# The rows of maxima turned by VectorE instead of TensorE, sent in eight transfers, with 24 tiles of exponentials and a new issue table

## The chip, the cores and the metric

One core of a Trainium2 chip runs the whole program in one launch. The metric is device time in microseconds, from the first to the last instruction with the little that lies around them. A run of this kernel repeats to within a few tenths of a microsecond; a difference of 0.2% (about 3.4 us) is the smallest that counts here.

## The reference, cut to what matters

```
xn  = layernorm(x)                                  # 2048 tokens x 512
q, k, v = split(xn @ wqkv)                          # 32 heads of 16
p   = softmax(q k^T / 4)                            # 2048 x 2048 per head, not causal
s   = (p v) @ wo
g   = silu( (silu(xn @ w1) * (xn @ w3)) @ w2 )      # 512 -> 1792 -> 512
out = x + s * g
```

All is float32. The weights are drawn large, so the scores are large, and the softmax needs each row's maximum taken off before the exponential.

## The kernel before, in words

**Shape of the work.** After a prologue (layer norm, q/k/v, some 160 us) the attention runs in 32 phases (`PHASES`): 16 pairs of heads, and for each pair two halves of 1024 queries. The gate (w1, w3, w2) is worked in between. Each operand that needs it is split in a high and a low part, and three products stand for one exact one. What a phase does:

- **maxima**, "m" (line 388): 64 products of 128 queries by 512 keys. VectorE reduces each to one maximum per query (line 390). A phase's maxima are needed one phase ahead, so they are worked out during the phase before.
- **rows**, `max_rows` (lines 393 to 414): the 16 columns of maxima of the phase (two heads by eight blocks of 128 queries, 128 partitions) have to become rows of `qs`, the tile that holds the queries: partition 62 of each half tile takes the negated maximum's high part, partition 63 its low part. The keys' tile holds ones there, so the next product takes the maximum off by itself.
- **exponentials**, "s" (line 626): 64 products of 128 keys by 512 queries, now with the rows of maxima in the contraction (64 partitions, `KR`; the maxima use 62, `KM`). ScalarE's Exp moves each to an SBUF tile `pt` (line 629), of which there are `PTS` = 23.
- **values**, "v" (line 639): four `pt` tiles times the values with a column of ones, added up in one PSUM bank `pv`. 16 of these in a phase.

**Lanes.** The products m, s and the gate's f (line 857) contract over 64 partitions. TensorE takes two at once, one on partitions 0 to 63 (lower-case letter, one head), the other on 64 to 127 (capital). Such a half product is one slot of a lane. A "v", an "o" of the end and the transpose of line 403 need the whole array, so both lanes have to end first.

**The order of the work** is written out by hand in `ORDER_OF_ISSUE` (lines 50 to 137), one letter for each step: m M s S f F for a half product in a lane, v for the values of one block of keys, o for a step of the output projection, r for "the transpose of the rows of maxima, then a v". Beside the letters a small clock in the program (`Model`, lines 232 to 295) keeps account of when each engine should be free; it decides which PSUM bank of seven is taken, when loads are issued, and whether a letter that comes too soon is put off (`late`, line 1245). All engines run their instructions in the order in which the program issues them.

**The rows in the old way.** `max_rows` is a generator that `small` (line 1163) steps on. Step 0, as soon as the last m of the phase is issued: VectorE reduces `mp` to `m` (128x16, line 396). Step 1: ScalarE negates it into `nm` (line 399). Step 2 waits for an "r" in the table, or `second` (line 1236): TensorE transposes `nm` into a PSUM bank (line 403), ScalarE rounds it to the high part `mh` (line 406), VectorE takes the low part `ml` (line 407), each of 16 partitions by 128. Step 3: four transfers of 4 KB on SyncE's queue write the four rows of 1024 (line 414), each from 8 partitions to one. `ready[phase]` (line 1173) tells `open_chunk` (line 1110) from when s of that phase may be issued: 3.5 us after the clock's time for `ml`.

**Other users of SyncE's queue** are nearly all transfers: the gate's weights (line 306), keys and queries of the next pair (lines 367, 376), the sums and shares of `take_out` (lines 651 to 675).

Of the kernel before, what the change touches and what calls it, by code (L numbers as in the profile page):

```python
# [9 lines left out]
F32 = mybir.dt.float32  # L10
# [7 lines left out]
P = 128  # L18
# [17 lines left out]
PTS = 23  # L36
# [19 lines left out]
    "msFFsfFFsFmsMvvsMSmMsvMmfMSfmMFvvMFssfMffSfMfSFfmSFffSmfFsFFmSfFFmsFfFFffMfSfMffSMfFFsmFfFmfSfFSfFmF"
    "sfFFmFsfSFsFmvrvvMsSffMFfSffMSffFmSSFffFmsFffMFSffMsFfsFMfFmFFfsmFmMvFvsMsMMsvMmsMfFSSfvSmMsMsvSmffS"
    "MffSFfMfSfMffSmsfFmSFfSfmsFfFSmFfFFmFsFmfSsFFfmFfSFfmFsFmSfFMfFffFmMMmvvMsfMfSMsvMssMMsvmSFfMsFsfFFm"
    "fFSmFsFfmFFsFfMsfFsFmFSfFfMfFsfSmFsFfFMfSffFMsFfMfFffMfMMffMMmvvvSmmMSmvvSmmSFfSffFFmsFFmFsFfFmSfSfF"
    "mfFfMSsfFFmfSfFmFsFFmFsfFFmSffFsFMffMMmvrfMFMsMmMfvvvfMSfMfSffSfMffSfMFsfmFFsFmSfsFfFFmfFmSfFFsFmFsF"  # L60
    "fmFsFFmsFFFmFssFSsvvSmsSsSvvSmSmmSvmSFmsFFfFsFmfSFfMsfFfSFmfSfFMfSfSfFmfMFfFFmMvvsMsMsfFfFmFfMsfFsFM"
    "ffSfFMfSfFmSfFsFfFfmMMsvrsMMssMvMsSfMffSFffMFfmSfSFfmFFsFfmFsFfMsFfFfFmSFmmMvvmSsMMmvvsMsFFmFmFsFfFs"
    "fFSmfFSfMfFfSfMffSfFSmfFFffFFMSffMfFSffSmfsMfsFFmFsFmFsFmFfFMfmFMmvvMsMmfSfSvmSsMSmvMsfMfSfFSffMFfmS"
    "fSFfFmFfsFmsFfFSFmfSfFmfFfFMSFfffFSFmsFfmFFmsFfsFSffMFFffmFFfMmMmvvvvmMSsMsvSmsFmFmFFsFsFfFfSmFfSfMf"
    "FffMSffFsMfFfFMffSFfFMfSfSfFMfsmsFfFmsFfFMsFmFfSfmFfFFmfMMmvvvmSMssSvrvSmmFsFsFmFFsfFFfMsfFfMfSfFfMS"
    "mfFfSfFfMFsfMFMsvvvmFsFmsFFmsFFffSfMfSFfmSfFmFsFMffFSfSfMmvmSMffMsSvsMSfSffMFfFfSmfFsFMfsFfFsMFfFmsF"
    "sFfMFfffFMfSffSFMffMsfSFfFmFsfFMsfFmFsFFfFmFmFmSmvvvSmsSsSvvSsMmMsvfSfMSfMfSffMfSfFfSfMFfsFFsmFfsFMf"
    "sFfFMsFfmFSFfffMFMfssMvsFSFMmMsvrvMsfSMfffSfMSffMFffSmssfFMFfsFmfFsFFmfSFmfFSffSFmSFfFmsFFfmFsFfMsFM"
    "fFffSmFSmvvSmMsMmvvmMSfmSSfvSmmSMsvSmsFFmsFFfFmSffFSmfFSfMfSffFMsfFMfsFFfMfsFfFsMFffSMfSffFsMFfmFFsm"
    "FfFFfFFMmMmvvvMssmFsFsFmFffFFsMfFsMfFfSffMSffMFffSmFfSfFfMSfFmSfFfFmSfFmfFFfMmmMvvrMsmFFfSsvvvSmsFFm"  # L70
    "FsfFFfFmSfmFfSfFFsmFmFfSFfFsmFFsFfmSfFmFsFFsfFfSSfMsvvSssSmMvvvFmsFmFsFmFsFfFsFFmSffFMsfFfMSfMffFMff"
    "MSsvMfmSMfSsvmSsMSmvmSfSMfSfFffMmFfSfsFmFfFSFfFsmFfSmFffSFffmFFMFfSfmFsfFFsMFfFsmFsfFMsfFmFSfFfMfFmS"
    "fMmvvmMsSMsvsMFmFsFsmFFfFsfFMsfFfMSfFfMfSffMFsfFfMmFfMMmvvvMmmSsMvrMsSffMFfSffMSfFfmSffFSmFsFfMsfFFF"
    "msFmmFfFFmMFmvvsMsMfFfSffMsFfMfFFsmFsFFfsFmSFffMfSfffFfMFfSMffSfMfFsFFmFsFmSffFFmFsFmFfFmmFsMvvSmSmS"
    "mvfMMsSfSmvmSmSSmvmSFmFsFfFsfMFsfMfFsFMffSFfmSFffMsFfMFfsMfFMmvvMmmMsSvrmSfSmFFfFsFmsFFsFmfFSMfSfFfm"
    "SfFMfSfFffMfMFmMsvvvsMMffSfFfSfMSffFsMFfsFmFFsfFsMFffMsFfFsFffFMfMfFSffSfMSffFmSfFfSmFsFfFmFsFmFFsFm"
    "FsmFvvvvsMSmFffFsFfFSmfFSfMfSffFmSfFmFsFFffMFFfmSSmvvvMsFsfMfsFfFMfsFfFFmsFMfsFMffFFsMfFffMfSsMvmSfS"
    "MfFffSfMSffFsMfFfSMffFSfFmsFfMFsFffMsFFfFsfFSsSmvvSmmFSSsvvvSmmSMsvSfMfSfMffSfFSfMffSfMsfFmFsfMfSFfF"
    "sFmFsfMFsfFMfsFFsfMFfFsFmsFfFMfsFfMsFMfFffFsSMmvmMsMmSvvmMsSMmvrmSfSMffSFffMSffFsMFfSfMffSFfmFsFmFfF"
    "FsFmsFfFmSfFFsFmFsFfmSFfmFsFfFfMfMSfmsMSSvmFmvmSSmmMvvmFMmFmMmvvvmFsFFmsFFsFmFffSmFSffMfSfFmFSfSffMf"  # L80
    "SFffMSffFMfFsfMSfFfFmsFMfFfsSfFmMvMssMsMvrsMsFFsFmFmFfFsFfmFFmSffFFsFmSffFSfmFSfmFSffFmFSfFmFfmFmFmS"
    "vvMmsSSmvsMmFFssFsFFmfFfFfMfSfMFsfFfMSfFmFfsFfMMmvFvMsMmSsvfMMfSsMsvMsfSffMSffMFffSFmmFSfffSMFfsfFmF"
    "fsfFmFFsFFfMFsFFfmsFFSfmfSFfMFfsFfmFSfFmFMffmFsMvvMsSsmMvSmmFMmFmvvrSmSfmFfFsFFmSffMFsFffMfSfMfSFsFf"
    "fMffFfFFMSffMfSfSfMfSfFmFsfmFSFfsmFFfsFFssFFsmFvvvvsMsMmSvMsFfsMSffFfMfSfMfFsMFfsSfFfMfFFsmFsFFfmFfF"
    "fMfFSfMfSfSfmFffSFmFFsmsFfFFmSFffFmFFmmSmvvmSmSmSvvmSMmMsvvsMsFFmFsFfFmFsFfMfFsfMSfMfFfSfMfFsfFfFMfS"
    "ffMfSfSfFMFfsmFsFfMsfFmFsFFfMfSfmFmFfFsFsMvvSfSfsMfSvvvsMMfSffFSffMsfFfMSfFsFFmsFfFmsFFFfsmFfFMfFfSm"
    "SfFFmFfSfmFfSmFSfFfFmsFFmfFSsFfsMvvvmSsSSsvvmSsMsSvrsMffSMSfFffMfSfFmSfSfFmFFsFfmfFSmFfFsFfFfmFfMSff"
    "FSmFsFfMfFsFmFsFSfmFsFfMfMfFFfFmmSmvvvMsmFfSFfsFFmfSFffMsFFsMfFffSMfSfFfMsfFMfSffMFffFMmmMvvvMsmmMff"
    "MvFvSfMfSMfSfffSMffSmSfFfMsfFFMfsFFsfMsfFFMfFsfMFsffFMsFsFfMfFsFmFsFFmsFfMfFMsfFmMvvvmSSFfmffSFfMfSf"
    "FmSffFSmfFFfSmsFFmFsfFFFmsfFSfMFsFfmfSfFMFsffMSfFfFFmsFmMsvvvrvfSMfSffMfSffSMfSFfmFSffMSfFffMsFFfsMf"  # L90
    "sFFsMFffSFmFfFsmFFsfFmSFfFmsFsfFFFsmFSsvvvSmSssSvvmSmSSmvSmFsSmFmvmSfFSmFsFfFmfFsFmFsFFmsFfFsFMffSFm"
    "SfFfmFSffMFssFFfSfsFMmvvSssMmSvvSsSsMmvvMsSmmSvMssFFmsFmFfFsFfMfSfFfMFsMffSfFfMsFfMFfmFFMfSmvvmSMssf"
    "FfFFmMfFsfFFsFmfFSmFFsfMFfMfffSMffSmSvmMmSSmvrsMmFSfFfFsFmFsfFMffSMffSMfFfSfFmsFfFFsFfSsMsvvvFFmsMfs"
    "SfFFffMSffFmfSMffFSfmFFsFsfFMfFFfMffSfMSffFFfSmfFsFmFsFmfSFfFmsFFmfFfMmFSFmvvmSsmFFsFfFfsMFfFsfMFsFf"
    "MsfFMfSfFfFmfSMfmSFvMmSsmMvvmMsMmMvvfSfMSffMfSfSfmFsFfFmFFsfMsFmFFfsFfFMmMfFfmSvvsMMsMsvmSfSMffFSffM"
    "SffFmSfsFFmFmfFSfFsFmSFfFfffmFFMSFfMfFfsFmsFfFFsmsFfFMsfFmFSfFfmFMsfSfMmvrvSmSmmsMvvMMSmvmFFsmFFssFm"
    "FFffSfMSffFmSFfMfsFfFMfsFSfMFmvMsFSmMsvMfMsMsfSFvssMSmfFfmSffFSmFFfsMSffFMfsFFmfSFffMfMFmmMvvvsMSfMf"
    "FffSfMfSFfmSfFfSFmFfFsmFfSFmfFsfFFmFfMfSfFSfmFSffFsFMfFssFmFfFmFsFMfFfFmSfsSvvvSmSmmMvrsMSfMfFfSffMf"
    "SFfmFsfFMssFfFMfSFfmFsFfMFsffMSFffMfFfsSMmvsSmMsFMvvvvMffSMfSffMfSffSfMfSfmSFfMfFsfMfFSsFfFmSfFfmFFs"
    "fMsFFffSFmSfFmsFfFFmsFsFfFmFFmMmvvMmsMMmvvFsFmsfFmFSfFFsmSffFFfMSfsFfMfFsFmFsfFFFmsfFSFmFfSfmFSffMsF"  # L100
    "ffFMMfMfffMFMfMmvvvMFsmfSffSfMfSffSMfFsFmFFsFfSmfFSfmFfFFsmFfFsMffFSFmSffFmSfFmFsFfFMfsFMfSmvMmmMSsv"
    "vmMSmMsvrSmFmFssFFsFmfFFfFsMfsFFmFffSFmFsmFfFsFFfMsfFfMSfFfFsFfSmSsFvvvvmFsFmFsFmFsfFfSFmFsFfMsfFMfS"
    "fSffFfMMfsMFvsMFMfSfsSvSmMfsfSffMmFfsFFfSFmSfFfmFsFfMfFFsFmSmvvSsFSmSmvFvmSMfSfFMmvvmSSmsffFmSfFfMsF"
    "fFsMFsFfsMfFfMfSfFFffMsMmMvvMsfMfSfFMffSfsFMfFSffMFsfmFsFfFSmfFfsFFmFfFFMSfffMsfFfFSmsFFmFsfFFsMFfFs"
# [1248 lines left out]
```

## Time and profile before

| | |
|---|---|
| median of 3 runs | 1724.45 us (1723.78 to 1724.91) |
| the profiled execution | 1724.77 us |
| its span, first to last instruction | 1723.0 us |
| granted TensorE clock | 1.00 |
| instructions | 35685 |

The sums of the prediction are made against the profiled execution's 1724.77 us; it lies 0.3 us above the median of the three runs, and 1.8 us of it lie outside the span. In the profile, PE is TensorE's matmuls, PEld its weight loads, DVE VectorE, ACT ScalarE, POOL GpSimd, SPq SyncE's queue. A matmul's duration in the trace overlaps with the next one's; the pace is read from the starts. "Idle before" is the time that an engine stood still ahead of an instruction, and the name behind the arrow is what ended it.

### The profile page before, as it was taken

The numbers are of one execution on the slowest core, as the hardware profiler recorded it, in microseconds if no ns is written. First come the engines' busy times: TensorE is split into PE (matmuls) and PEld (weight loads), VectorE is DVE, ScalarE is ACT, GpSimd is POOL, SyncE is SP. The second block draws the span as 40 slices with busy tenths as digits, with TensorE's granted clock in tenths as the row PEclk, the third lists the DMA queues.
The fourth block names the chain that finished last, engine by engine and source line by source line (L and its number), as shares of the span: only waits on it lengthen the run. The fifth ranks groups of instructions, "written<-read, shape, count | busy, mean of one in ns | idle before, by whom it ended". The sixth has DMA issues, their size and how long they took to land.

```text
span 1723.0 us, 35685 instructions
## 1 busy us (share of the span) xinstructions
PE 1715.4 (100%) x13236; PEld 1099.0 (64%) x13236; DVE 1418.7 (82%) x2349; ACT 1240.6 (72%) x2440; POOL 766.5 (44%) x793
## 2 busy tenths in 40 slices
PE   9999999999999999999999999999999999999998
PEld 7877766666556666666666666656666666564466
DVE  7567989898889889888789897799878888888835
ACT  4223787778877787787887778777787778778952
POOL 4102744365546542654464706661666156621201
PEclk9999999999999999999999999999999999999999
DMA  8757213232332312233322303133413223130632
GB/s 282 248 204 206 65 46 66 53 70 64 73 113 59 66 53 61 55 66 95 100 64 55 80 19 91 57 75 94 94 53 67 57 66 94 30 112 20 214 121 99
DMA packets 147374, 155.37 MB, mean 90 GB/s; under 512 B 42368, under 2 KB 101760, under 8 KB 144224
## 3 DMA queue, kind: packets, MB, share of 16 engines
q1 hardware_dynamic: 146336, 152.04, 32.2%
q8 instruction: 104, 1.70, 0.4%
q10 hardware_dynamic: 864, 1.05, 0.2%
q14 instruction: 70, 0.57, 0.1%
HBM read 107.97 MB, written 44.02 MB: 88 GB/s over the span
## 4 chain that ended last, share of the span: by engine, by line
PE 98%; DVE 1%; DMA 0%; issue 0%; POOL 0%; ACT 0%; SPq 0%; DVEq 0%; ACTq 0%; POOLq 0%
PE f L857 28%; PE pv L639 28%; PE m L388 16%; PE e L626 16%; PE m L506 2%; PE e L194 2%; PE e L198 2%; PE e L196 2%; PE o L194 1%; PE o L198 1%; PE o L196 1%; PE m L479 0%; PE m L403 0%; DMA qs<-ml 0%; PE o L1088 0%; DVE wr L1035 0%
## 5 line engine op out<-in xcount | busy, mean ns | idle before, releaser
L390 DVE TENSOR_REDUCE mp<-m 128x1 f32<-128x512 f32 x2048 | 1287.1, 683 | 204.3 <-PE m L388 130.0
L629 ACT ACTIVATE pt<-e 128x512 f32<-128x512 f32 x2048 | 1072.3, 606 | 280.0 <-PE e L626 161.2
L626 PE MATMUL e<-qs,ks 64*128 64x512 f32 x2048 | 709.0, 408 | 0.6 <-DMA qs<-ml 0.5
L388 PE MATMUL m<-ks,qs 62*128 62x512 f32 x2048 | 708.2, 416 | 0.1
L639 PE MATMUL pv<-pt,vt 128*17 128x512 f32 x4096 | 497.4, 595 | 0.0
L388 PEld LDWEIGHTS m<-ks,qs 62*128 62x128 f32 x2048 | 334.4, 184 | 158.7 <-DVE mp L390 52.5
L626 PEld LDWEIGHTS e<-qs,ks 64*128 64x128 f32 x2048 | 343.1, 184 | 125.8 <-DVE mp L390 33.7
L639 PEld LDWEIGHTS pv<-pt,vt 128*17 128x17 f32 x4096 | 90.2, 96 | 220.0 <-issue 210.2
L857 PE MATMUL f<-xth,wh 64*128 64x512 f32 x488 | 175.4, 392 | 0.0
L857 PE MATMUL f<-xtl,wh 64*128 64x512 f32 x488 | 174.6, 392 | 0.0
L857 PE MATMUL f<-xth,wl 64*128 64x512 f32 x488 | 173.2, 394 | 0.0
L742 POOL TENSOR_TENSOR h<-g,h 128x512 f32<-128x512 f32 x56 | 72.2, 1289 | 187.7 <-ACT h L738 187.6
L857 PE MATMUL f<-wh,hs 64*128 64x512 f32 x496 | 153.7, 393 | 0.0
L857 PE MATMUL f<-xtl,xeh 64*128 64x512 f32 x408 | 148.9, 392 | 0.0
L857 PE MATMUL f<-xth,xel 64*128 64x512 f32 x408 | 145.8, 395 | 0.0
L857 PE MATMUL f<-xth,xeh 64*128 64x512 f32 x408 | 142.4, 391 | 0.0
L857 PE MATMUL f<-xeh,hs 64*128 64x512 f32 x400 | 127.6, 393 | 0.0
L321 POOL TENSOR_TENSOR wl<-wr,wh 128x512 fp32r<-128x512 f32 x92 | 118.6, 1290 | 7.7
L320 POOL TENSOR_SCALAR wh<-wr 128x512 fp32r<-128x512 f32 x92 | 57.3, 622 | 121.2 <-PE f L857 61.2
L321 POOL TENSOR_TENSOR xel<-wr,xeh 128x512 fp32r<-128x512 f32 x76 | 98.0, 1290 | 6.3
L857 PEld LDWEIGHTS f<-xth,wl 64*128 64x128 f32 x488 | 85.4, 185 | 7.3 <-issue 3.4
L857 PEld LDWEIGHTS f<-xth,wh 64*128 64x128 f32 x488 | 86.9, 185 | 4.9 <-issue 0.8
(184 smaller groups left out, 2007.6 us busy)
## 6 DMA issues: line engine op xcount, KB each, us to landing
wr<-in_B_w_dram SPq DMA_DIRECT2D x168, 256.0 KB
qs<-qk SPq DMA_DIRECT2D x186, 64.0 KB
ks<-qk SPq DMA_DIRECT2D x90, 128.0 KB
qk<-sh SPq DMA_DIRECT2D x32, 256.0 KB
qk<-sl SPq DMA_DIRECT2D x32, 256.0 KB
v<-vrow SPq DMA_DIRECT2D x16, 272.0 KB
xin<-in_A_x_dram SPq DMA_DIRECT2D x16, 256.0 KB
g<-part SPq DMA_DIRECT2D x16, 256.0 KB
```

The lines of the kernel that those rows point to most:

```text
L194: nc.tensor.matmul(ps, lhs[1], rhs[0], start=first, stop=False)
L196: nc.tensor.matmul(ps, lhs[0], rhs[1], start=False, stop=False)
L198: nc.tensor.matmul(ps, lhs[0], rhs[0], start=False, stop=last)
L320: nc.gpsimd.tensor_scalar(hi, t, 1.0, 1.0, op0=ALU.mult, op1=ALU.mult)
L321: nc.gpsimd.tensor_sub(lo, t, raw(hi))
L388: nc.tensor.matmul(ps, qs[p % 2][64 * h:64 * h + KM, q0:q0 + P], ks[p % 2][64 * h:64 * h + KM, c * 512:(c + 1) * 512], start=True, stop=True)
L390: nc.vector.reduce_max(mp[p, half][:, h, qt, c:c + 1], ps, axis=AX.X)
L626: nc.tensor.matmul(ps, ks[p % 2][64 * h:64 * h + KR, k * P:(k + 1) * P], qs[p % 2][64 * h:64 * h + KR, q0:q0 + 512], start=True, stop=True)
L629: nc.scalar.activation(pt, ps, AF.Exp, scale=DH ** -0.5)
L639: nc.tensor.matmul(pv[32 * j:32 * j + VW, :], vt[2 * p // GH][:, key, 2 * p % GH + j % 2, :], pt, start=key < 2 if last else k == 0, stop= ...
L742: nc.gpsimd.tensor_mul(h2, g, h2)
L857: nc.tensor.matmul(ps, left[r], right[r], start=starts and lane == 0, stop=ends and lane == 1)
```

## The change: what it does

- In `max_rows` ScalarE writes the negated maxima straight as the rounded high part `hi`, into every other group of eight columns of a 128x32 tile `both`. VectorE then takes the low part `lo` = -m - hi in one instruction (scalar_tensor_tensor, 128x16) into the other groups, and turns `both` in blocks of 32 by 32 into `turned` (VectorE's transpose, 128x32). The transpose of TensorE with its PSUM bank, the copy to `mh` and the subtraction to `ml` go.
- A block turned this way leaves each 32 queries' maxima in its own 32 partitions, so the rows are brought by eight transfers instead of four: for each head and each of four blocks, 16 partitions by 32 numbers go to two rows of `qs`, eight pieces of 128 bytes in each.
- `small` steps through without waiting for a letter; `second` goes, and so do the letters r and R. Step 2 is VectorE's two instructions, step 3 the transfers, and `ready` becomes 6.0 us after the moment at which these are issued.
- The room of `mh` and `ml` goes to one more tile of exponentials: `PTS` 23 becomes 24. It is the bound in `exponentials` (line 1129) on how far s may run ahead of v.
- The table is new throughout: 8598 letters instead of 8599. Both have 2016 each of f and F, 1024 each of s and S, 992 each of m and M, 22 o; 482 v, 30 r and one R become 512 v.

```
-PTS = 23
+PTS = 24
...
-        nm = keep.tile([P, 16], F32, tag="nm", name="nm", bufs=2)
+        both = keep.tile([P, 32], F32R, tag="nm", name="nm", bufs=2)
+        hi, lo = (both.rearrange("p (h n q) -> p h n q", h=2, n=2)[:, :, n, :] for n in range(2))
+        m = m.rearrange("p (h q) -> p h q", h=2)
         yield
-        nc.scalar.activation(nm, m, AF.Copy, scale=-1.0)
+        nc.scalar.activation(hi, m, AF.Copy, scale=-1.0)
         yield
-        i, ps = take("m")
-        begins = mod.whole(0.1, was_free[i] + mod.NOTICE)
-        nc.tensor.transpose(ps[:16, :P], nm, ident)
-        mh = keep.tile([16, P], F32R, tag="mh", name="mh", bufs=2)
-        ml = keep.tile([16, P], F32R, tag="ml", name="ml", bufs=2)
-        nc.scalar.copy(mh, ps[:16, :P])
-        nc.vector.tensor_sub(ml, ps[:16, :P], raw(mh))
-        free_at[i] = mod.work("dve", mod.work("act", begins + 0.5, 0.25), 0.28)
+        nc.vector.scalar_tensor_tensor(lo, m, -1.0, raw(hi), op0=ALU.mult, op1=ALU.subtract)
+        turned = keep.tile([P, 32], F32R, tag="nt", name="nt", bufs=2)
+        nc.vector.transpose(raw(turned), raw(both))
         yield
         c = slice(half * 1024, (half + 1) * 1024)
         for h in range(2):
-            for n, v in enumerate((mh, ml)):
-                r = 64 * h + KM + n
-                nc.sync.dma_start(raw(qs[p % 2])[r:r + 1, c], raw(v)[8 * h:8 * h + 8, :])
+            r = 64 * h + KM
+            to = raw(qs[p % 2])[r:r + 2, c].rearrange("n (q b i) -> n q b i", q=8, b=4)
+            for b in range(4):
+                nc.sync.dma_start(to[:, :, b, :], raw(turned)[32 * b + 16 * h:32 * b + 16 * h + 16, :])
...
-    def small(due=False):
+    def small():
...
-            if c[2] == 2 and not due or c[2] != 2 and c[0] > mod.now:
+            if c[0] > mod.now:
                 continue
             if c[2] == 0:
                 c[0] = mod.work("dve", mod.now, 0.25)
             elif c[2] == 1:
-                c[0] = mod.work("act", c[0], 0.2) + 1.0
+                c[0] = mod.work("act", c[0], 0.2)
+            elif c[2] == 2:
+                c[0] = mod.work("dve", mod.now, 0.4)
             if next(c[1], "end") == "end":
-                ready[c[3]] = mod.free["dve"] + 3.5
+                ready[c[3]] = mod.now + 6.0
                 rows.remove(c)
-            elif c[2] == 2:
-                c[0] = mod.now
             c[2] += 1
...
-        if c in "rR":
-            second()
-        if c in "rv":
+        if c == "v":
...
-        elif c != "R":
+        else:
             what = (c.lower(), int(c.isupper()))
```

More of the change, by code (lines that the diff above doesn't have):

```diff
@@ L56 @@
[L56 to L80, printed above, removed]
@@ L137 @@
+    "MSsSMossSMsvMsSmvSSmsSSmMvSMssMSmvMssSSMmvsMsSmMvMSsMSSsSmvsMsmvMsMsMsvMMssMsSvMsmSsMosSSssSooosSsSS"
+    "svvsSSssSvvvsSSsSssvvvoSossSsSovoSsSssSvvSsSssSoSssSsSvvsSsSsSoosSsSSsvvvsSsSSsoooSsSsSoooooovvvvv"
 )
@@ L1234, in half_issued @@
         return ok
-    def second():
-        while rows and rows[0][2] < 2:
-            rows[0][0] = 0.0
-            small()
-        if rows:
-            small(True)
     late = []
@@ L1279 @@
         tend()
-        if rows and rows[0][2] == 2 and rows[0][0] <= mod.now:
-            second()
         if values_ready(mod.now):
```

145 lines of the change are left out of this document (84 added, 61 removed).

## The prediction, made before the result was known

> **What bounds the kernel now.** I read the head of the page and the chain that ended last, then the costliest groups, then the timeline.
>
> ```profile
> span 1723.0 us, 35685 instructions
> ...
> PE 1715.4 (100%) x13236; PEld 1099.0 (64%) x13236; DVE 1418.7 (82%) x2349; ACT 1240.6 (72%) x2440; POOL 766.5 (44%) x793
> ...
> PE 98%; DVE 1%; DMA 0%; issue 0%; POOL 0%; ACT 0%; SPq 0%; DVEq 0%; ACTq 0%; POOLq 0%
> ...
> L390 DVE TENSOR_REDUCE mp<-m 128x1 f32<-128x512 f32 x2048 | 1287.1, 683 | 204.3 <-PE m L388 130.0
> ...
> L626 PE MATMUL e<-qs,ks 64*128 64x512 f32 x2048 | 709.0, 408 | 0.6 <-DMA qs<-ml 0.5
> L388 PE MATMUL m<-ks,qs 62*128 62x512 f32 x2048 | 708.2, 416 | 0.1
> L639 PE MATMUL pv<-pt,vt 128*17 128x512 f32 x4096 | 497.4, 595 | 0.0
> ```
>
> The chain is TensorE's for 98%. The last column is the point: before its 2048 exponential products TensorE stood idle 0.6 us in all, before the maxima 0.1, before the values 0. VectorE, the next busiest, stood idle 204.3 us before its reductions, 130.0 of them until a maxima product came. So VectorE waits for TensorE and not the other way round.
>
> The busy share alone would not prove this, since ends are modelled. The starts do:
>
> ```profile
> 1008.13 0.40 PE L857 MATMUL f<-xeh,hs 64*128 64x512 f32 x1
> 1008.20 0.39 PE L626 MATMUL e<-qs,ks 64*128 64x512 f32 x1
> 1008.36 0.39 PE L857 MATMUL f<-xel,hs 64*128 64x512 f32 x1
> 1008.43 0.42 PE L388 MATMUL m<-ks,qs 62*128 62x512 f32 x1
> ```
>
> Each lane starts a product every 0.23 us, without a hole. What leaves TensorE's stream shortens the run; what is added elsewhere costs only if TensorE comes to wait for it.
>
> **Term 1: the transpose goes.** Two neighbouring values steps, and the same two with the transpose of line 403 between them:
>
> ```profile
> 901.44 1.91 PE L639 MATMUL pv<-pt,vt 128*17 128x512 f32 x16
> ...
> 576.51 1.05 PE L639 MATMUL pv<-pt,vt 128*17 128x512 f32 x8
> 577.50 0.28 PE L403 MATMUL m<-ident,nm 128*16 128x128 f32 x1
> 577.71 1.05 PE L639 MATMUL pv<-pt,vt 128*17 128x512 f32 x8
> ...
> L403 PE MATMUL m<-ident,nm 128*16 128x128 f32 x32 | 8.9, 277 | 0.0
> ```
>
> Two steps alone take 1.91 us; with the transpose 577.71 + 1.05 - 576.51 = 2.25. The difference, 0.34 us, is more than the 0.277 us of the group's mean. Of the 32 transposes, 29 stand between two values steps: 29 x 0.34 = 9.9 us. The other three:
>
> ```profile
> 1593.38 0.38 PE L626 MATMUL e<-qs,ks 64*128 64x512 f32 x1
> 1593.69 0.28 PE L403 MATMUL m<-ident,nm 128*16 128x128 f32 x1
> 1593.90 1.05 PE L639 MATMUL pv<-pt,vt 128*17 128x512 f32 x8
> ...
> 1639.36 0.39 PE L198 MATMUL o<-ks,xth 128*128 128x512 f32 x1
> 1639.59 0.27 PE L403 MATMUL m<-ident,nm 128*16 128x128 f32 x1
> 1639.62 0.48 PE L194 MATMUL o<-ks,xtl 128*128 128x512 f32 x1
> 1639.93 0.39 PE L196 MATMUL o<-wh,xth 128*128 128x512 f32 x1
> ```
>
> The first holds the values up by 1593.90 - 1593.69 = 0.21. Between whole-array products it costs 1639.93 - 1639.36 - 2 x 0.23 = 0.11, twice with the prologue's. **Together -10.3 us.** Nothing else was waiting in its shadow: those 0.34 us lie in a stream without holes.
>
> **Term 2: the table.** Between two whole-array steps the fuller lane sets the length. Counting the letters, the fuller lane's slots sum to 4119 in the old table and 4110 in the new: 9 x 0.23 = -2.1 us. Runs of v, each of which drains the lanes once, fall from 275 to 273. One drain costs about 0.2 us (1593.69 - 1593.38 = 0.31 in the rows above, where the next start of the two lanes would have come after 0.12): -0.4 us. Both are counts of text, exact only if letters are not put off. **Together -2.5 us;** bounds 0 and -5.
>
> **Term 3: the small instructions.**
>
> ```profile
> L407 DVE TENSOR_TENSOR ml<-m,mh 16x128 fp32r<-16x128 f32 x32 | 8.7, 273 | 9.0 <-ACT mh L406 8.8
> L406 ACT CAST mh<-m 16x128 fp32r<-16x128 f32 x32 | 8.1, 252 | 16.4 <-PE m L403 16.1
> L396 DVE TENSOR_REDUCE mx<-mp 128x16 f32<-128x64 f32 x32 | 7.0, 220 | 1.1
> L653 DVE RECIPROCAL rec<-sums 128x16 f32<-128x16 f32 x29 | 6.9, 238 | 0.0
> ```
>
> ScalarE loses 8.1 us. VectorE loses the 0.273 us of line 407 and gains a 128x16 operation (nearest rows 0.22 and 0.24) and a 32 by 32 transpose of 128x32, which no row shows: bounds 0.22 (the 128x16 reduction) and 0.68 (a whole 128x512 reduction, line 390). I take 0.25, near line 407's 0.273, which runs over four times its columns. So +0.2 us x 32 = +6.4 us on VectorE, and 0.6 us x 32 = 20 at the upper bound, both under its 204.3 us of idle time. Cost 0. The new wait is VectorE's for `hi` from ScalarE; behind it stand reductions that free PSUM banks, and TensorE waits for those. The same wait exists today (`ml` for `mh`, 8.8 us in all) and TensorE's idle time is still 0.6. If that cover went, 8.8 us is the price.
>
> [...]
>
> **Term 4: the rows come later.** This is the term that can undo the rest. Old transfers, their queue and the first product that used them:
>
> ```profile
> 935.61 0.70 SPq L414 DMA_DIRECT2D qs<-mh  x1
> 936.41 0.67 SPq L414 DMA_DIRECT2D qs<-ml  x1
> 937.13 0.62 SPq L414 DMA_DIRECT2D qs<-mh  x1
> 937.80 0.62 SPq L414 DMA_DIRECT2D qs<-ml  x1
> ...
> 787.67 2.48 SPq L651 DMA_DIRECT2D sums<-ot  x4
> ...
> 939.80 0.72 PE L626 MATMUL e<-qs,ks 64*128 64x512 f32 x2
> ```
>
> Four issues stand 0.73 us apart (935.61 to 937.80 over 3), and the rows had landed 2.0 us after the last. The other transfers within SBUF with short runs (64 bytes, line 651) stand 0.62 apart. The new ones, 16 partitions with runs of 128 bytes, are in no row: bounds 0.62 and the longest issue of line 414, 1.25. I take 0.62 to 0.73, the two nearest.
>
> ```profile
> L414 SPq DMA_DIRECT2D qs<-ml x64: 623/634/1248, 157.7 to 1642.8; - x64
> ...
> L396 DVE TENSOR_REDUCE mx<-mp x32: 207/220/222, 150.7 to 1636.0; 128x16 f32<-128x64 f32 x32
> L399 ACT ACTIVATE nm<-mx x32: 209/217/262, 150.9 to 1637.4; 128x16 f32<-128x16 f32 x32
> ```
>
> From the start of `mx` to the first product of the phase the new chain needs: 0.6 until ScalarE gets to it (first 0.2, last 1.4 of 32), 0.2 its work, 0.4 in VectorE's queue (about half a reduction), 0.5 for its two instructions, 0.1 to SyncE, 7 more issues, 2.0 to land. That is 3.8 + 7 x 0.62 = **8.1 us**, or 3.8 + 7 x 0.73 = **8.9 us**.
>
> What it gets I read off the new table: the time from the last m of a phase (32 in each lane) to its first s, at 0.116 us a half product, 0.86 us a v, 0.22 us a run of v. The same count on the old table can be held against the profile, for the first phase and the last but one:
>
> ```profile
> 204.58 0.22 DVE L396 TENSOR_REDUCE mx<-mp 128x16 f32<-128x64 f32 x1
> 215.83 0.39 PE L626 MATMUL e<-qs,ks 64*128 64x512 f32 x1
> ...
> 1591.14 0.22 DVE L396 TENSOR_REDUCE mx<-mp 128x16 f32<-128x64 f32 x1
> 1600.05 0.40 PE L626 MATMUL e<-qs,ks 64*128 64x512 f32 x2
> ```
>
> Phase 1: 11.2 us measured, 12.4 counted. Phase 30: 8.9 measured, 8.3 counted. So the count holds to about 1 us. In the new table the shortest are phase 3 with 6.6, 1 with 7.4, 22 with 8.9, 4 with 9.1, 30 with 9.5; then 10.5, 10.6, 11.0, 11.1, 12.0, 12.2, 12.2, 12.3, and the other eighteen from 13.3 up. The program's clock puts off an s that comes earlier than about 7.1 us (by the constants in `small` and `work`: 0.33 for the reduction, 0.3 for ScalarE, 0.5 for VectorE, then 6.0), so phase 3 has 7.1. At 8.9 needed, phases 3 and 1 wait 1.8 + 1.5 = 3.3 us, at 8.1 they wait 1.0 + 0.7 = 1.7. **I take +2.5 us.** SyncE's queue is held 4 x 0.7 = 2.8 us longer in each phase; behind it stand the gate's weights, split five units ahead, so I cost that at nothing.
>
> The 24th tile lets s run one further ahead of v. TensorE waits for no tile now, so 0.
>
> **Sum:** 1724.8 - 10.3 - 2.5 + 2.5 = 1714.5 us, against the profiled execution's own time, 1723.0 of span and 1.8 around it. The median of the runs is 0.3 lower, which is less than the terms are good for: **1714.5**.
>
> **The rivals.** (a) *The rows come too late in many phases: slower.* With issues 1.25 us apart the chain needs 3.8 + 8.75 = 12.55 us, and thirteen phases fall short of it: 5.4 + 5.1 + 3.7 + 3.4 + 3.1 + 2.0 + 2.0 + 1.6 + 1.5 + 1.5 = 29.3 us (the last number is four phases together). 1724.8 - 12.8 + 29.3 = 1741. It decides at a need of 10.85 us, where the shortfalls sum to 12.8: a spacing of 1.0 us. For it: eight issues in one queue in order, short runs. Against: every row of that queue's short transfers lies at 0.62 to 0.73. Between the forecast and this lie 1719 to 1728.
>
> (b) *VectorE is the bound: slower.* Then TensorE's transpose is worth nothing and VectorE's 6.4 us come on top: 1731. For it: its 82% busy share and reductions in rows without a break. Against: the 130.0 us that it waits for maxima products. [...]
>
> (c) *The rows are always in time*, and the lighter ScalarE and the 24th tile let lanes fill better: 1712.0 without term 4, down to 1708 if term 2 doubles. For it: the old table's waits on rows sum to 0.5 us. Against: the two short gaps above.
>
> **How the numbers follow.** The forecast (1712.5 to 1719) has 0.59, (c) 0.10, the middle ground up to 1728 0.10, (a) in full 0.15, (b) 0.06. A measurement tells 0.2%, 3.4 us, from no change. Faster: 0.59 + 0.10 + 0.03 of the middle = 0.72. Same: 0.07 of the middle + 0.02 of (b) = 0.09. Slower: 0.15 + 0.04 = 0.19. The range 1709 to 1729 leaves out most of (a), some of (b) and the end of (c), 0.19 together.
>
> **What would show it.** Right: no matmul between two values steps, each such pair 1.91 us; TensorE's idle time before exponential products 2 to 3 us, by the new transfers, in phases 1 and 3; issues 0.6 to 0.75 us apart. Wrong: idle time before line 626 of over 10 us, or spread over many phases (term 4); issues of 1 us and more; VectorE's transpose above 0.7 us; idle time before maxima products that VectorE ends (term 3).

## The result, and the profile after

The changed kernel takes 1727.93 us (1725.03 to 1730.46, 11 runs), the kernel before beside it 1723.2. The ratio is 1.0025, 95% interval [1.0016, 1.0034]: 4.3 us slower, where 9.9 us faster was forecast. The profiled execution is the slowest of the 11, 1730.46 us. Its page, with the lines that answer to those of before:

```profile
span 1728.7 us, 35745 instructions
...
PE 1717.1 (99%) x13204; PEld 1098.9 (64%) x13204; DVE 1425.6 (82%) x2381; ACT 1234.9 (71%) x2408; POOL 764.7 (44%) x793
...
PE 96%; POOL 1%; SPq 1%; DVE 1%; DMA 1%; issue 1%; ACT 0%; ACTq 0%; DVEq 0%; POOLq 0%
...
L390 DVE TENSOR_REDUCE mp<-m 128x1 f32<-128x512 f32 x2048 | 1285.5, 683 | 202.7 <-PE m L388 124.7
...
L624 PE MATMUL e<-qs,ks 64*128 64x512 f32 x2048 | 717.2, 411 | 3.9 <-DMA qs<-nt 2.1
L388 PE MATMUL m<-ks,qs 62*128 62x512 f32 x2048 | 711.3, 417 | 0.7 <-DVE mp L390 0.7
```

TensorE still ends nearly everything, but 4% of the chain is other engines' now, and it stands idle 3.9 us before exponentials (0.6 before) and 0.7 before maxima. Idle time alone doesn't make up the difference. The mean duration of the same product is up too, 411 ns instead of 408. The windows (time, busy us of PE, PEld, DVE, ACT, POOL, then the granted clock) say why:

```profile
150.00:200.00 50.00, 46.09 (x312) 32.90 (x310) 33.66 (x57) 26.32 (x51) 20.64 (x22) 0.93 0.43 125
200.00:250.00 50.00, 50.00 (x414) 31.07 (x408) 43.45 (x74) 37.24 (x72) 28.85 (x30) 1.00 0.15 41
250.00:300.00 50.00, 48.54 (x387) 32.92 (x385) 36.41 (x61) 40.17 (x78) 27.32 (x29) 0.97 0.31 73
...
1600.00:1650.00 50.00, 49.30 (x299) 24.10 (x300) 39.67 (x65) 36.60 (x73) 9.59 (x10) 0.97 0.66 212
```

Three windows have a mean clock under 1, apart from the run's last, which has it in both kernels. In each of the three TensorE also stood idle. Before, these windows show 1.00. The first is the end of the prologue. Its timeline, SyncE's queue, ScalarE and TensorE together:

```profile
158.60 5.43 SPq L412 DMA_DIRECT2D qs<-nt  x8
...
165.04 0.40 SPq L510 DMA_DIRECT2D v<-vrow  x1
...
165.18 0.47 PE L624 MATMUL e<-qs,ks 64*128 64x512 f32 x1 [2.10 <-DMA qs<-nt]
...
167.98 2.56 ACT L627 ACTIVATE pt<-e 128x512 f32<-128x512 f32 x5 [4.83 <-DVE mp L390]
...
168.63 0.79 PE L624 MATMUL e<-qs,ks 64*128 64x512 f32 x1 [1.81 <-ACT pt L627]
...
169.65 0.62 PE L388 MATMUL m<-ks,qs 62*128 62x512 f32 x1
170.07 0.62 PE L624 MATMUL e<-qs,ks 64*128 64x512 f32 x1
170.50 0.62 PE L388 MATMUL m<-ks,qs 62*128 62x512 f32 x1
```

Phase 0's eight issues hold SyncE's queue for 5.43 us. TensorE waits 2.10 us for the rows, then 1.81 for ScalarE, whose first exponential comes 4.83 us after its last work. After that a lane's starts lie 0.42 to 0.43 us apart instead of 0.23: half clock, 0.50 in the clock's record for 6.8 us (167.62 to 174.45). The second window has one wait for GpSimd, the third one for VectorE, and each of these is followed by a half-clock stretch of 3.4 us (0.50 from 287.09 to 290.50 and from 1621.70 to 1625.11):

```profile
286.17 0.49 PE L855 MATMUL f<-xeh,hs 64*128 64x512 f32 x1 [1.46 <-POOL hs L742]
...
1619.61 0.49 PE L388 MATMUL m<-ks,qs 62*128 62x512 f32 x1 [0.70 <-DVE mp L390]
```

### The profile page after: what moved, and what is told of

It reads as the page before. It is cut to its first block, busy times and chain, and to the rows that moved or that the text cites. A ratio compares the mean times of both kernels' runs of the same rounds, so it can differ in the third digit from the quotient of the medians.

```text
span 1728.7 us, 35745 instructions
## 1 busy us (share of the span) xinstructions
PE 1717.1 (99%) x13204; PEld 1098.9 (64%) x13204; DVE 1425.6 (82%) x2381; ACT 1234.9 (71%) x2408; POOL 764.7 (44%) x793
## 4 chain that ended last, share of the span: by engine, by line
PE 96%; POOL 1%; SPq 1%; DVE 1%; DMA 1%; issue 1%; ACT 0%; ACTq 0%; DVEq 0%; POOLq 0%
PE f L855 27%; PE pv L637 27%; PE m L388 16%; PE e L624 15%; PE m L504 2%; PE e L194 2%; PE e L198 2%; PE e L196 2%; PE o L194 1%; PE o L198 1%; PE o L196 1%; SPq L412 1%; PE m L477 0%; DMA wl<-o 0%; ACT pt L627 0%
## 5 line engine op out<-in xcount | busy, mean ns | idle before, releaser
L390 DVE TENSOR_REDUCE mp<-m 128x1 f32<-128x512 f32 x2048 | 1285.5, 683 | 202.7 <-PE m L388 124.7
L624 PE MATMUL e<-qs,ks 64*128 64x512 f32 x2048 | 717.2, 411 | 3.9 <-DMA qs<-nt 2.1
L388 PEld LDWEIGHTS m<-ks,qs 62*128 62x128 f32 x2048 | 338.4, 185 | 154.8 <-DVE mp L390 51.9
L855 PE MATMUL f<-xth,wh 64*128 64x512 f32 x488 | 171.7, 393 | 0.0
L855 PE MATMUL f<-xth,xeh 64*128 64x512 f32 x408 | 146.1, 395 | 0.0
L855 PE MATMUL f<-wl,hs 64*128 64x512 f32 x248 | 92.8, 395 | 0.0
L724 POOL TENSOR_SCALAR th<-th 128x512 f32<-128x512 f32 x56 | 34.6, 618 | 129.7 <-ACT th L717 129.4
```

The lines of the kernel that those rows point to most:

```text
L388: nc.tensor.matmul(ps, qs[p % 2][64 * h:64 * h + KM, q0:q0 + P], ks[p % 2][64 * h:64 * h + KM, c * 512:(c + 1) * 512], start=True, stop=True)
L390: nc.vector.reduce_max(mp[p, half][:, h, qt, c:c + 1], ps, axis=AX.X)
L624: nc.tensor.matmul(ps, ks[p % 2][64 * h:64 * h + KR, k * P:(k + 1) * P], qs[p % 2][64 * h:64 * h + KR, q0:q0 + 512], start=True, stop=True)
L855: nc.tensor.matmul(ps, left[r], right[r], start=starts and lane == 0, stop=ends and lane == 1)
```

## The experiments

Ratios are to the kernel before, run beside each on the same chip; its medians were 1723.1 to 1723.5.

**The changed kernel again** (no edit).

> The changed kernel once more, unaltered, to see which of the three stalls of its first profile are its own and which came by chance. Theory A (the loss is three stalls, the largest at phase 0, where eight transfers hold SyncE's queue 2.7 us longer, each followed by a TensorE clock halved for 3.4 to 6.8 us): the stall at 162 to 174 us comes back with 4 to 5 us of idle time and a halved clock after it; the two at 284 and 1618 us may or may not. Time 1725 to 1730. Rival B (the new table is worse all along): the values steps fall behind those of the kernel before steadily, not in three places.

1728.66 us, 1.0030 [1.0018, 1.0041]. The wait at the end of the prologue and the one near 285 us come back in the same places, each again with a half-clock stretch, of 6.8 and 3.4 us. The wait for VectorE near 1619 us comes back too (0.73 us), this time without one; the mean clock of the run is 0.997, where the first profile has 0.996. The places of the waits belong to the kernel.

**Phase 0's rows by TensorE**, as before, in tiles of the prologue's second pool; the other 31 phases as changed.

```
-        first_rows = max_rows(0, 0)
+        first_rows = rows_by_tensor(0, 0)      # transpose, mh, ml, four transfers
```

> The changed kernel with phase 0's rows alone made in the old way (TensorE's transpose, four transfers); phases 1 to 31 and the table stay new. Theory A: the stall at phase 0 goes with its halved clock, 6 to 7 us; 1720.5 to 1722, below the kernel before. Rival B (the table): no change against the changed kernel, 1727 to 1728. Rival C (the clock is lower for another reason, such as the denser stream): granted clock still 0.997 and below, time within 2 us of the changed kernel.

1725.77 us, 1.0011 [1.0002, 1.0020]: 2 to 3 us come back, not 6 to 7. The wait for rows was gone, but one of 1.45 us at 165.4 us was left, put down to the first exponential, and the first product of the lanes still came 1.5 us later than before (161.86 us, not 160.38).

**The kernel before, phase 0's four transfers cut into eight.**

```
+                if p == half == 0:
+                    for e in range(2):
+                        nc.sync.dma_start(raw(qs[p % 2])[r:r + 1, 512 * e:512 * e + 512],
+                                          raw(v)[8 * h + 4 * e:8 * h + 4 * e + 4, :])
+                    continue
```

> The kernel before with one part of the change alone: phase 0's four row transfers cut into eight halves, all else as before. Theory A: rows and the three stores behind them come 2.5 us later, TensorE waits there, the clock halves; 4 to 7 us slower, 1727 to 1730. Rivals B and C: no more than the 2.5 us of the wait itself, or nothing, 1723 to 1726.

1725.59 us, 1.0012 [1.0003, 1.0020]. This lies in the range of rivals B and C, 1723 to 1726: about the length of the wait and no more. In the profiled run TensorE waits 1.36 us for the rows at 161.5 and the clock stays at 1.0. Eight issues in this one phase cost about 2 us without any of the rest of the change.

**The kernel before with four stalls put into TensorE's stream** (a copy on VectorE, a transfer and a transpose that waits for it, at four points).

```
+        if count["V"] in (130, 210, 290, 370):
+            nc.vector.tensor_copy(one, c["pts"][0][:, 0:16])
+            nc.sync.dma_start(two, one)
+            nc.tensor.transpose(ps[:16, :P], two, ident)
```

> The kernel before with four stalls of TensorE put in, at values steps 130, 210, 290 and 370: VectorE copies 16 columns of a tile of exponentials, a transfer copies them on, and TensorE transposes the copy into a bank that nobody reads. The disputed price by itself. Theory A: each stall of about 3 us is followed by some microseconds at half clock, so that the four cost 4 x (3 + 1.7 to 3.4) = 19 to 26 us, 1742 to 1749, granted clock 0.99. Rival C (a stall does not lower the clock): 4 x 3 = 12 us, 1735, granted clock 1.00.

1746.27 us, 1.0130 [1.0116, 1.0143], 23 us more. The windows of two of the stalls, then the timeline at the first:

```profile
550.00:600.00 50.00, 46.02 (x357) 29.55 (x355) 39.86 (x68) 34.54 (x69) 26.46 (x27) 0.93 0.29 64
...
800.00:850.00 50.00, 45.43 (x359) 29.98 (x359) 37.56 (x64) 30.99 (x61) 17.20 (x18) 0.93 0.30 82
```

```profile
577.01 0.37 PE L1205 MATMUL m<-ident,two 128*16 128x128 f32 x1 [3.98 <-DMA two<-one]
577.32 3.62 PE L639 MATMUL pv<-pt,vt 128*17 128x512 f32 x16
```

Two steps of values take 3.62 us behind the stall, 1.91 elsewhere. The four idle times sum to 14.5 us (3.99 + 4.57 + 3.09 + 2.85). Behind them lie half-clock stretches of 6.8, 6.8, 3.4 and 3.4 us; half of these 20.4 us, or 10.2, is a little more than the 8.6 us that are still missing. The run's mean clock is 0.994, where the kernel before has 1.000. So the low clock is an effect of a stall and not its cause. Shorter stalls bring such a stretch in some executions and not in others: 0.70 us near 1619 us did in the first profile of the changed kernel, 0.73 us didn't in the second. GpSimd's wait near 285 us is followed by a stretch of 3.4 us in both of these profiles, in the first after 1.46 us of idle time. In two kernels that come further down, both with phase 0's rows by TensorE, it is as long and no stretch follows: 1.5 us with the prologue placed (mean clock of that run 1.000), 1.40 us with the pools apart (1.00 in the window from 250 to 300 us). The kernel with phase 0's rows by TensorE took 1723.3 to 1724.2 us in the runs with a mean clock of 1.000, and 1724.9 to 1728.5 in those with 0.999 or 0.998.

**Placement.** The change frees 1664 bytes in the pool that lies lowest and adds 2048 above, so everything between moves. The first try at undoing this, for the changed kernel and for the one with phase 0's rows by TensorE:

```
     with tc.tile_pool(name="pro", bufs=1) as pro, tc.tile_pool(name="pros", bufs=1) as pros:
+        pro.tile([P, 416], F32, name="low")
+        pros.tile([P, 64], F32, name="gap")
```

> The changed kernel with two unused tiles that move the prologue's tiles back up: 1664 bytes below the prologue's weights, so that they lie at the addresses they have in the kernel before, and 256 bytes below the rows that v is stored from, so that the stage after the prologue has no tile over them. No instruction is changed. Theory A (placement: in the changed kernel the products of the projections start 231 ns apart instead of 227, and the first exponential waits for the store of v because its pool reaches over that tile): the first product of the lanes comes 1.5 to 2 us earlier, the wait of 4.83 us before the first exponential falls to about 2 to 3 (what the rows of phase 0 leave), and the median falls from 1728 to 1723 to 1726. Theory B (placement does nothing): 1727 to 1730, and the products of the projections stay 231 ns apart.

> The kernel with phase 0's rows turned by TensorE, with the same two unused tiles. Theory A (placement): prologue 1.5 to 2 us earlier, the 2.09 us wait of the first exponential for the store of v gone: 1721.5 to 1723 instead of 1725.8, with a granted clock of 1.000 in more of the runs. Theory B (placement does nothing): 1725 to 1727.

1726.13 us, 1.0013 [1.0004, 1.0023], and 1721.35 us, 0.9991 [0.9982, 1.0000]. A row of the groups (the last number before the bar's end is the mean ns of one product of the projections), in the changed kernel and in the placed one:

```profile
L196 PE MATMUL e<-xtl,wqh 128*128 128x512 f32 x64 | 25.2, 394 | 0.0
```

```profile
L196 PE MATMUL e<-xtl,wqh 128*128 128x512 f32 x64 | 25.0, 390 | 0.0
```

390 is also the number before. The starts move by the same 4 ns, 231 and 227, and over the prologue's products this is the 2 us. So where the operands lie made the prologue slower, with the same instructions. The other half of the forecast failed, because the second tile was put into the wrong place: the first exponential waits as ever.

```profile
162.86 3.05 ACT L653 ACTIVATE pt<-e 128x512 f32<-128x512 f32 x6 [2.24 <-DMA v<-vrow]
```

**The kernel before, moved by 384 bytes**, which gives the prologue's weights the changed kernel's address modulo 2048.

```
     rows2 = [keep.tile([P, KC, 512], F32R, name=f"ov{v}2") for v in "hl"]
+    keep.tile([P, 96], F32, name="low")
```

> The kernel before with one unused tile of 384 bytes ahead of the prologue's tiles, which puts the weights of the prologue at an address that equals that of the changed kernel modulo 2048 (105632 becomes 106016; the changed kernel has 103968). No instruction is changed. Theory A (the address alone slows the prologue's products from 227 to 231 ns): the first product of the lanes 1.5 to 2 us later, median 1724.7 to 1725.5. Theory B (it was something else of the changed kernel): 1723.0 to 1723.5 and 227 ns.

1725.13 us, 1.0007 [0.9998, 1.0016], but the same product takes 390 ns. So it isn't the weights' address modulo 2048 alone. What about the address makes the 4 ns stays open, and so does whether the 1.7 us here are real.

**Pools apart.** The 256 bytes in a pool of their own between the prologue's two, in both kernels.

```
+ tc.tile_pool(name="gap", bufs=1) as gap   # between pro and pros
+        gap.tile([P, 64], F32, name="gap")
```

> As the placed kernel with phase 0's rows by TensorE, but the 256 unused bytes lie in a pool of their own between the prologue's two pools, so that the stage after the prologue lies over no byte of the second pool. Theory A (a new pool waits for every tile of an old pool that it overlaps, so the first exponential waited 2.24 us for the store of v): that wait falls to about 0.3 us, the 1.46 us of idle TensorE at 163.5 is gone, median 1719.3 to 1720 instead of 1721.35. Theory B (the first exponential waits for the store of v for another reason): 1721 to 1722 and the wait stays.

> The changed kernel with the same placement, nothing else. Theory A (pools): the first exponential no longer waits for the store of v behind the eight transfers; TensorE keeps the wait of 2.26 us for phase 0's rows at 162.4 and loses the one of 1.85 us at 165.9, and with it perhaps the half-clock stretch of 6.8 us: 1723 to 1725 instead of 1726.1. Theory B: 1726 to 1727.

Phase 0 by TensorE: 1719.91 us, **0.9983 [0.9975, 0.9992]**, faster than both kernels. The changed kernel: 1722.40 us, 0.9999 [0.9990, 1.0008]. The first exponential, to be held against the row above:

```profile
160.75 3.05 ACT L653 ACTIVATE pt<-e 128x512 f32<-128x512 f32 x6 [0.31 <-PE f L881]
```

The tile that v is stored from lies at the same address in both, and no tile of the next stage lies over it in either; only whether the *pools* overlap differs. So the wait was for the old pool, whatever was in it. Of the changed kernel's loss, 1.0025 - 0.9999, or 4.5 us, was placement: 2.1 came with the prologue's addresses (1.0025 to 1.0013) and 2.4 with the pools (1.0013 to 0.9999). Each ratio is known to about 0.0009 either way, so such differences to some 2 us. What phase 0's eight transfers cost by themselves is the difference of the two kernels of this experiment, 0.0016 or 2.8 us: in the profile of the second, TensorE still waits 2.25 us for the rows at 162.6 us, with a half-clock stretch of 3.4 us behind it.

**The first part of the change alone:** phase 0's rows by TensorE, the prologue placed as in the first try, VectorE's transposes in the other 31 phases, but the table of before (r read as v) and 23 tiles. The first exponential does not wait here (0.33 us at 160.80).

> Phase 0's rows by TensorE, all others turned by VectorE with eight transfers, prologue placed as before, but the issue table of the kernel before (its letters for the transposes taken as plain value products) and 23 tiles of exponentials: the change's first part alone. Theory A (the transposes' 9.5 us are gained, and what ate them are stalls tied to the new order): 1714 to 1717. Theory B (eight transfers that hold SyncE's queue and late rows cost in any order): 1719 to 1723. Theory C (the old order, made for other durations, stalls more than it gains): over 1724.

1724.47 us, 1.0004 [0.9996, 1.0013]: theory C's end. 31 of the 32 transposes are gone from TensorE, and nothing is gained. Before and this kernel, at a place where the gain stays and at one where it doesn't:

```profile
403.57 1.05 PE L639 MATMUL pv<-pt,vt 128*17 128x512 f32 x8
404.56 0.28 PE L403 MATMUL m<-ident,nm 128*16 128x128 f32 x1
404.76 1.91 PE L639 MATMUL pv<-pt,vt 128*17 128x512 f32 x16
406.61 0.50 PE L626 MATMUL e<-qs,ks 64*128 64x512 f32 x1
```

```profile
402.97 2.77 PE L663 MATMUL pv<-pt,vt 128*17 128x512 f32 x24
405.67 0.49 PE L650 MATMUL e<-qs,ks 64*128 64x512 f32 x1
...
1453.88 0.39 PE L881 MATMUL f<-xth,xel 64*128 64x512 f32 x1
1454.12 0.50 PE L881 MATMUL f<-xtl,xeh 64*128 64x512 f32 x1
1454.12 1.09 PE L650 MATMUL e<-qs,ks 64*128 64x512 f32 x2
1454.71 0.49 PE L881 MATMUL f<-xth,xeh 64*128 64x512 f32 x1
1454.71 0.18 PEld L650 LDWEIGHTS e<-qs,ks 64*128 64x128 f32 x1 [0.41 <-DVE mp L390]
...
1452.81 3.64 DVE L390 TENSOR_REDUCE mp<-m 128x1 f32<-128x512 f32 x6
```

406.61 - 403.57 = 3.04 us become 405.67 - 402.97 = 2.70: the forecast's 0.34. At 1454 the lane's next start comes 0.59 us after the last one instead of 0.23, while VectorE works off six reductions without a break, each of which frees a PSUM bank; the load that waits for such a bank is the row with 0.41 in brackets. Over the 31 phases the values right behind the old transpose come 0.32 us sooner on average, and six steps later only 0.16.

The order of the products is nearly that of before: 542 of the 554 stretches between TensorE's whole-array steps hold the same products, and no product waits for rows. So the loss isn't from letters put off. The largest single one, 1.1 us at 531 us, begins at the new instruction on VectorE that makes the rows:

```profile
530.50 1.28 POOL L321 TENSOR_TENSOR wl<-wr,wh 128x512 fp32r<-128x512 f32 x1
...
530.57 1.24 DVE L403 SCALAR_TENSOR_TENSOR nm<-mx,nm 128x16 fp32r<-128x16 f32 x1
...
531.98 5.43 DVE L390 TENSOR_REDUCE mp<-m 128x1 f32<-128x512 f32 x9
...
532.68 0.49 PE L650 MATMUL e<-qs,ks 64*128 64x512 f32 x1 [0.41 <-DVE mp L390]
```

It takes 1.24 us instead of 0.17 and ends when GpSimd's instruction does; nine reductions pile up behind it, and TensorE waits for them. Of the 31 instructions of this kind in the profile, 11 took over 0.2 us (0.27 to 1.24, one of them ahead of the reductions at 1454), and each of these ends 0.02 to 0.04 us after an instruction of GpSimd that was running when it began. The changed kernel shows the same. The two-operand instruction of before, `ml`, took 0.27 to 0.28 us every time. No run tells apart how much of what is lost comes from this and how much from the banks as such.

The wait view of the weight loads, before, then this kernel:

```profile
PEld m L388 <- DVE mp L390: 52.5, 80, 0.9
...
PEld e L626 <- DVE mp L390: 33.7, 49, 0.9
...
PEld m L403 <- DVE mp L390: 10.2, 12, 0.9
```

```profile
PEld m L388 <- DVE mp L390: 59.8, 92, 0.9
...
PEld e L650 <- DVE mp L390: 38.8, 63, 0.9
```

The loads of the maxima and exponentials wait more for VectorE, 86.2 us in 129 waits before and 98.6 in 155 after. But the transposes' own loads waited 10.2 us in 12, so the sum of before is 96.4 in 141. For the most part the waits moved from the transposes to the products behind them, which is what a transpose that hid in a wait would do; the sum doesn't show the loss, and a product still running hides an unknown part of each wait.

**The transfers alone:** the kernel before with its table and its transposes, the four transfers of every phase cut into eight.

```
-                nc.sync.dma_start(raw(qs[p % 2])[r:r + 1, c], raw(v)[8 * h:8 * h + 8, :])
+                for e in range(2):
+                    c = slice(half * 1024 + e * 512, half * 1024 + (e + 1) * 512)
+                    nc.sync.dma_start(raw(qs[p % 2])[r:r + 1, c], raw(v)[8 * h + 4 * e:8 * h + 4 * e + 4, :])
```

> The kernel before, with its transposes on TensorE and its table, but the four transfers of every phase cut into eight: the cost of the transfers alone. Theory A (the rows come up to 2.6 us later and SyncE's queue is held as much longer in each of 32 phases; this is where a part of the gain went): phase 0 gives 1.5 to 2.4 as in the run that cut it alone, and phases 1, 3 and some others 0.3 to 1 us each, 1726 to 1729. Theory B (outside phase 0 the eight transfers are hidden): 1724.5 to 1726, as with phase 0 alone (1725.6).

1732.99 us, 1.0056 [1.0043, 1.0069], 9.7 us: more than both theories. The wait view has six waits for rows,

```profile
PE e L628 <- DMA qs<-ml: 4.6, 6, 1.4
```

and five of the six waits lie outside phase 0 (266, 322, 1568 and two at 1654 us). In the old order the rows had little time to spare in these places. The waits are 4.6 of the 9.7 us, a half-clock stretch of 3.4 us behind the first adds 1.7, and a wait for VectorE 1.1; the rest isn't told apart. These transfers also differ in form from the change's: each reads from 4 partitions where the change's read from 16, so their price need not be that of the change's.

**The 24th tile:** the fastest kernel so far, with `PTS` = 23.

> p0_old_apart with 23 tiles of exponentials instead of 24 and the same new table. Theory A (the 24th tile is worth nothing, as the prediction put it): 1719.5 to 1720.5. Theory B (the new table relies on it; with 23 tiles letters are put off and the products come in 289 stretches instead of 279, the fuller lane in 4083 slots instead of 4073, 10 times 0.23 us): 1722 to 1726.

1728.30 us, 1.0028 [1.0019, 1.0037]: 8 us slower than with 24, more than theory B asked. The prologue's products take 390 ns here and the first exponential waits 0.33 us, so the placement is not what made it slower. The old table with 24 tiles wasn't run.

**Phase 0's rows from two queues:** the changed kernel with pools apart, every other of phase 0's transfers issued by ScalarE.

```
+                queue = nc.scalar if p == half == 0 and b % 2 else nc.sync
```

> after_apart (the changed kernel with its pools apart), and of phase 0's eight row transfers four are issued by ScalarE, which is idle there for over 2 us at a time. Theory A (phase 0's rows are late by the time that eight issues take on SyncE's queue, 5.4 us): the rows are issued by 158.8 instead of 161.4, TensorE's wait of 2.25 us at 162.6 goes, no half-clock stretch behind it, and the median falls from 1722.4 to 1719.3 to 1720.5, the time with phase 0's rows by TensorE. Theory B (the transfers themselves are slow, whoever issues them): 1722 to 1723.

1727.75 us, 1.0023 [1.0013, 1.0033]. Worse, and by neither theory:

```profile
146.40 10.75 SPq L376 DMA_DIRECT2D qs<-qk  x3
...
163.04 2.82 SPq L413 DMA_DIRECT2D qs<-nt  x4
...
167.00 0.76 PE L627 MATMUL e<-qs,ks 64*128 64x512 f32 x1 [6.04 <-DMA qs<-nt]
```

Three loads ahead of the rows on SyncE's queue now hold it for 10.75 us, until after ScalarE has begun its four at 155.04, and the second four come at 163.04. TensorE waits 6.04 us for the rows, and 6.8 us at half clock follow. Why the loads wait isn't shown, and the question of the issuing time is left to the difference of 2.8 us above.

**GpSimd's wait near 280 us.** Two splits of attention's output moved to VectorE, first in phase 1, then one of them in phase 0.

```
+        eng = nc.vector if (p, half) == (0, 0) else nc.gpsimd
-        nc.gpsimd.tensor_sub(ol, ot, raw(oh))
+        eng.tensor_sub(ol, ot, raw(oh))
```

> p0_old_apart, and in phase 1 alone the two splits of the attention's output (0.62 and 1.29 us on GpSimd) go to VectorE. Theory A (TensorE's wait of 1.46 us for GpSimd's hs at 279 us comes from these 1.9 us ahead of four weight splits on GpSimd): the wait is gone, 1717.5 to 1718.5. Theory B (another piece of work takes its place, or VectorE's maxima come late by as much): 1719 to 1720.

> p0_old_apart, and in phase 0 alone the low part of the attention's output (1.29 us on GpSimd) is subtracted by VectorE. Theory A (these 1.29 us ahead of four weight splits make GpSimd's hs late at 277 us): TensorE's wait there falls from 1.40 us to about 0.1, 1718 to 1718.7. Theory B (the wait is refilled by the next piece of work, or VectorE's maxima come late): 1719.5 to 1720.5.

1720.40 us, 0.9981 [0.9972, 0.9990], and 1719.47 us, 0.9976 [0.9965, 0.9986]: no difference from 0.9983. The first edit missed, since the output being split at 264 us is phase 0's; TensorE waits for GpSimd as before. The second hit, and theory B holds:

```profile
264.93 1.09 DVE L689 TENSOR_TENSOR ol<-ot,oh 128x512 fp32r<-128x512 f32 x1 [2.07 <-POOL oh L688]
265.94 4.40 DVE L390 TENSOR_REDUCE mp<-m 128x1 f32<-128x512 f32 x7
```

The wait for `hs` is gone, but VectorE stands 2.07 us waiting in order for GpSimd's `oh`, seven reductions pile up behind, and TensorE waits 1.35 us for them at 266.7 instead.

## Why the prediction was wrong, step by step

**Term 1 (the transpose goes, -10.3): nearly right in size, wrong as a gain.** The time of values and transposes, added up from start to start, fell by 9.5 us, from 482.9 to 473.4, in the old order as in the new. But that is not a gain of the run: the half products between them grew from 1016.6 us by 11.1 in the old order and by 4.9 in the kernel with its pools apart and phase 0's rows by TensorE. The step that failed is "What leaves TensorE's stream shortens the run". With the old order kept, the run then took 1724.47 us, where the kernel before takes 1723.5. TensorE's idle time of 0.6 us shows that it never waited, not that it could have gone faster. What it came up against is seen at single places, VectorE's reductions and the banks they free (531 and 1454 us above); that the whole 11.1 us is this isn't shown. Of the 4.9 us, 2.1 are GpSimd's wait near 285 us.

**Term 2 (the table, -2.5): near in size by chance, wrong in its working.** By the products as issued, the fuller lane has 4073 slots in both kernels, so the 2.1 us of slots weren't there: letters that are put off change the count, which is the condition that the text named. Table and tile together are still worth 1.0004 - 0.9983, or 3.6 us. But with 23 tiles, as the old table has them, the new table makes the kernel 4 us slower (1.0028 against 1.0004). What the new order does is another thing than what I counted.

**Term 3 (small instructions, 0): the usual durations were right, the longest ones and the cover weren't.** VectorE's two instructions:

```profile
L405 DVE STREAM_TRANSPOSE nt<-nm x32: 211/211/214, 153.2 to 1643.6; 128x32 f32<-128x32 f32 x32
...
L403 DVE SCALAR_TENSOR_TENSOR nm<-mx,nm x32: 161/177/989, 153.0 to 1643.4; 128x16 fp32r<-128x16 f32 x32
```

The medians are 0.21 and 0.18 us, where 0.25 and 0.22 to 0.24 were taken. But the second takes up to 0.99 us, 0.335 on average, where GpSimd is at work beside it: VectorE gains 8.8 us of work instead of 6.4. Its cover, the 204.3 us in which VectorE is idle, is an average over the run; in a burst of reductions there is none. The sign that the prediction named for this, idle time before maxima that VectorE ends, did come: 0.7 us, where before had 0.1.

**Term 4 (rows later, +2.5): the spacing was right, the place was missed.**

```profile
L412 SPq DMA_DIRECT2D qs<-nt x256: 598/610/814, 158.6 to 1648.5; - x128
```

The median issue takes 0.61 us, a little under the lower of the two bounds that were taken, 0.62 and 0.73; phase 0's eight hold the queue for 5.43 us, 0.68 each, which lies between them. The count had phases 1 and 3 wait. In the kernel with its pools apart and phase 0's rows by TensorE, the stretches at 209, 317 and 354 us (phases 1, 3 and 4) take 0.89, 0.80 and 0.68 us longer than their products need, where 0.25 is usual: some 1.6 us together. But the profile names the rows for one wait only, 0.22 us at 211.7, so that the rows are the cause is not shown for the rest. And the count was made on the table, and phase 0's rows aren't in the table. They are issued by the prologue, between stores on the same queue, and they cost 2.8 us. "SyncE's queue is held 4 x 0.7 = 2.8 us longer in each phase ... so I cost that at nothing" is the sentence that failed: phase 0's own rows came late, TensorE waited 2.10 us for them, and while the pools overlapped, the store of v behind them on the queue held up the first exponential. In the old order, too, there was little slack (six waits of 4.6 us in all).

**"The 24th tile ... so 0" failed twice.** The new table is worth 8 us less without it; why is not known. And with the smaller tiles of the rows it moved the pools: 4.5 us, the largest single term of the error, and none of the prediction's terms looked at an address.

**What the forecast had no term for:** GpSimd's wait near 280 us (1.46 us here, and 2.1 in the time of its stretch of products), which the profiles of the kernels with the new table show, except the one whose split was moved off GpSimd in phase 0; and the half clock, which adds 1.7 or 3.4 us (half of a stretch of 3.4 or 6.8) to some stalls.

From the forecast's -9.9 us to the measured +4.3 the way is 14.2 us. Placement is 4.5 of it, phase 0's rows 2.8. GpSimd's wait is 2.1 by the profile. The remaining 4.8 us are not told apart further. The transposes' time that came back in the products behind them is among them; that small waits for banks took it back is argued from the places above. The kernel with its pools apart and phase 0's rows by TensorE, which stands at 0.9983, also has a wait of 1.61 us for `xtl` at 1630 us in its profile.

**The rivals.** (a) named the right place with the wrong price: the rows were not late in many phases of the changed order; in the old order six waits, 4.6 us, come close to it. (b) fails as it stood, since VectorE is idle for 202.7 us before its reductions in the changed kernel too. Yet the engine that it names is the one whose reductions TensorE caught up with at 531 and 1454 us. The waits of the weight loads for VectorE, 96.4 us before and 98.6 with the old order kept, hardly bear the rival out in sum. What the loads' wait view could have shown before the run is that TensorE had caught up with VectorE in 141 places; I read only that of the products. It would not have given the price.

## What to carry to other kernels

A bound engine that never waits is not proof that its time can be taken out: look at what its loads wait for, at how lately the buffers behind its stream came free, and run the removal alone, with the order of everything else kept. Look at the longest duration of a new instruction and not only at its median. Count a moved step in every place that issues it, the prologue too, and name what is queued behind it. When a change alters the size of any buffer, first run it with the old addresses and with the old neighbours of its pools.

## What the runs showed of the hardware that was not expected

- A stall of TensorE can cost more than its length. Stretches at half clock, 3.4 or 6.8 us long, follow stalls of 0.70 to 6.04 us in some executions; four stalls of 14.5 us in all cost 23.
- The same product takes 390 or 394 ns by where its operands lie, with starts 227 or 231 ns apart. 1664 bytes make this difference and 384 bytes don't; the rule behind it is open.
- VectorE's transpose of a 128x32 tile in blocks of 32 by 32 takes 211 ns, no more than a small reduction (220 ns).
- VectorE's instruction with two input tiles (128x16, usually 161 to 177 ns) took up to 1.24 us when GpSimd was at work as it began, and then ended within 0.04 us after GpSimd's instruction. The transpose of one tile beside it never took more than 0.214 us in the changed kernel.
